# Four crossed groups per pair in the second FFN, with a new order of its steps

## The chip, the cores and the metric

One core of one Trainium2 chip runs the whole program in one launch. The metric is device time in microseconds (us). The kernel before has a median of 1088.23 us over 3 runs (1087.71 to 1088.48).

## The reference

```python
qn = q / (norm(q, axis=1) + 1e-6);  kn = k / (norm(k, axis=1) + 1e-6)
a  = softmax(kn.T @ qn / tau)            # 256 x 256
x  = v @ a                               # 6016 x 256
g  = x @ w_gate                          # first FFN, 256 -> 1536 -> 256
x  = (g * sigmoid(g) * (x @ w_val)) @ w_out
h  = x @ w_in                            # second FFN, 256 -> 2048 -> 256
y  = (h * clip(h + 3, 0, 6) / 6) @ w_out2
```

## The kernel before, in words

Attention is folded into the first FFN's weights, and both FFNs run transposed, with features on the partitions and tokens along the free dimension. Tokens go in six pairs of two blocks. In the second FFN (layer two) a block has 512 tokens in five pairs and 448 in the last. All products keep about fp32 precision by splitting each operand into a high and a low part: one product is three matmuls (`mm3`, L114: high by high, low by high, high by low).

**The forward products.** Layer two has 16 tiles of 128 hidden features, which are taken two at a time: eight groups (0 to 7) per pair. A group is a 2x2 block product (two feature tiles by two token blocks, over two halves of the 256 inputs), done by the Strassen-Winograd scheme in seven products instead of eight: 21 matmuls into three PSUM banks, `ps_a`, `ps_b` and `ps_d`. ScalarE (ACT) copies `ps_a` into `ps_b` (step AB) and two intermediate sums to SBUF (steps D, B). VectorE (DVE) adds into these (A22, A12). Then for each of the four results ACT takes relu(x+3) (R11, R21, R22, R12) and DVE a clip times x (K11, K21, K22, K12). That is 7 ACT and 6 DVE instructions. The next group's products wait for these banks: `ps_a` for K11, `ps_d` for A12, `ps_b` for K21; and within a group P6 and P2 wait for AB, P7 for B, P3 for D, P4 for A22.

**The back products.** Each result is split for the second matrix: ACT writes the high part (H), DVE the low part (L), both in a place `hl` or `hx`. In a *plain* group, four results each meet 2 output tiles: 4 items of 6 matmuls into the accumulators `o`. In a *crossed* group the back product is a Winograd scheme as well, 7 items of 3 matmuls: DVE makes four differences (D1 to D4; three stay in `xt`), and there are seven splits (P1 to P7). P2, P3 and P4 go into `o`. P1, P5, P6 and P7 go into a shared bank `al`, one kind after the other for all crossed groups of the pair: all P1, an ACT copy (step C) of the running sum, all P6, a copy, all P5, a copy, all P7, a copy. So this chain can only end after the last crossed group. Then two DVE sums, and four DVE outputs `xo` (L1761) with their stores.

So a plain group has 45 matmuls, 10 DVE and 11 ACT instructions; a crossed one 42 matmuls, 17 DVE and 14 ACT. Per pair there are also 2 DVE sums, 4 DVE outputs, 4 ACT copies, and (except in the last pair) the preparation of the next pair's operands with 11 DVE and 7 ACT instructions. Before, groups 1 and 4 are crossed.

**The order.** Tile placement and order are written out by the program itself at build time. In layer two every instruction is a `Step` with an engine, needs, a place it takes, and a due time; `run_steps` walks a clock per engine at fixed rates and lets the engine take the startable step that is due first. On TensorE (PE) it decides between the next forward product and a back item by the rules in `pick` (how crowded DVE is, how much back work is waiting). SP issues the DMAs in the order found. The weights of the forward products come by DMA from a DRAM copy into a ring of three tiles, each with two groups.

**Before layer two.** In layer one the second FFN's weights are split and written to DRAM (`second_steps`, one step of the conversion beside each group of layer one, mostly on POOL). A crossed group's rows of the last matrix need Winograd sums there.

Of the kernel before, what the change touches and what calls it, by code (L numbers as in the profile page):

```python
# [18 lines left out]
def channel_attention_then_two_ffns(  # L19
# [24 lines left out]
    nc = tc.nc  # L44
# [13 lines left out]
    CROSSED = (1, 4)  # L58
# [409 lines left out]
    with tc.manual_schedule():  # L468
# [381 lines left out]
        class Cube:  # L850
# [151 lines left out]
        def cross_tile(j):  # L1002
            return room["t"][:, j]
# [25 lines left out]
        def shared_copy(name, p, n):  # L1029
# [4 lines left out]
                "P6": ((0, 1), cross_tile(NQ - 1)[:, :n]),  # L1034
# [11 lines left out]
        def cross_back():  # L1046
# [4 lines left out]
            w = room["w"][:, i]  # L1051
# [65 lines left out]
        NG2I = NF2 // CT // 2  # L1117
# [8 lines left out]
        plain_f = [CT * i + j for i in range(NF2 // CT) if i not in CROSSED for j in range(CT)]  # L1126

        def load_w2o(fs, pool, tag, size):
            t = pool.tile([P, size, 2, C], F32R, tag=tag, name="w2o")
# [9 lines left out]

        def next_weights(g):  # L1140

            if g < RING:
                load_w2i(g)
            elif g == RING:
                load_w2o(plain_f[:NQ], w1_p, f"w{g}", NQ)
                t = const.tile([P, HALF, TB], F32R, tag="wo0", name="hx")
                room["hl"] = [t[:, CT * j : CT * (j + 1)] for j in range(HALF // CT)]
            elif g == 4:
                room["w"] = w1_p.tile([P, len(CROSSED), 2, NQ, P], F32R, tag=f"w{g}", name="w2x")
                nc.sync.dma_start(out=room["w"].bitcast(F32), in_=wx_d)  # L1150
            elif g == 5:
                room["t"] = w1_p.tile([P, NQ, TB], F32, tag=f"w{g}", name="xt")
            else:
                room["e"] = [e_p.tile([P, TB], F32, tag="e", name="xe") for _ in range(CT)]
                load_w2o(plain_f[NQ:], const, "wo1", HALF)
# [225 lines left out]

        RATE = {"PE": (1.25, 40, 170), "ACT": (1 / 1.2, 95, 190), "DVE": (1 / 0.96, 72, 80)}
        LANDS = {"weights": 9000, "raw": 5500, "store": 4500, "operand": 5500, "out": 4500}
        GAP, PE_GAP = 130, 300
        queues = {e: [] for e in ("PE", "ACT", "DVE", "SP")}

        class Step:
            def __init__(self, engine, due, run, needs=(), takes=None, gives=(), n=TB, cost=1, ahead=None):
                self.engine, self.due, self.run = engine, due, run
                self.needs = [x for x in needs if x]  # L1390
                self.takes, self.gives, self.n, self.cost, self.ahead = takes, gives, n, cost, ahead
                self.end = None
                queues[engine].append(self)

        class Place:

            def __init__(self, kind, make, after=()):
                self.kind, self.make, self.tile, self.after = kind, make, None, [x for x in after if x]
# [7 lines left out]
        spare = {"h": [], "hl": []}  # L1406

        def passed_by(x, engine, t):
            if x.end is None or x.engine == engine == "PE":
                return x.end is not None  # L1410
            return x.end + (0 if x.engine == engine else PE_GAP if engine == "PE" else GAP) <= t

        def place_of(step, t):
            return next((q for q in spare[step.takes] if all(passed_by(x, step.engine, t) for x in q.after)), None)

        def can_start(step, t):
            if not all(passed_by(x, step.engine, t) for x in step.needs):
                return False
            return not step.takes or place_of(step, t) is not None

        def pick(engine, t):
            found = [s for s in queues[engine][:120] if can_start(s, t)]
            if engine != "PE":
                return min(found, key=lambda s: s.due) if found else None
            forward = next((s for s in queues[engine] if s.ahead is not None), None)
            items = [s for s in found if s.ahead is None]
            if forward not in found:
                return min(items, key=lambda s: s.due) if items else None
            crowd = sum(1 for s in queues["DVE"][:120] if s.due < forward.due + SOON and can_start(s, t))
            if items and (crowd >= BUSY or sum(s.cost for s in items) >= MOST):  # L1430
                return min(items, key=lambda s: s.due)
            return forward

        SOON, BUSY, MOST = 20000, 2, 10

        def run_steps():
            clock = {e: 0 for e in queues}
            while any(queues.values()):
                engine = min((e for e in queues if queues[e]), key=lambda e: clock[e])
                t = clock[engine]  # L1440
                step = pick(engine, t)
                if not step:
                    clock[engine] += 40
                    assert t < 2_000_000, [(e, len(q)) for e, q in queues.items()]
                    continue
                queues[engine].remove(step)
                if step.takes:
                    place = step.place = place_of(step, t)
                    spare[step.takes].remove(place)
                    step.run(place.get())  # L1450
                else:
                    step.run()
                for other in step.gives:
                    place = other.place
                    place.after = [step]
                    spare[place.kind].append(place)
                if engine == "SP":
                    busy, more = 60, LANDS[step.n]
                else:
                    rate, fixed, more = RATE[engine]  # L1460
                    busy = (rate * step.n + fixed) * step.cost
                clock[engine] = t + busy
                step.end = t + busy + more
                step.began = t

        def layer2():
# [9 lines left out]

# [5 lines left out]
            def old_item(entry, needs=()):  # L1482
# [9 lines left out]
                step = Step("PE", -5000 + len(l1_items), run, needs, cost=2, n=prev.n)  # L1492
# [10 lines left out]
            def old_split(h, key, needs, due):  # L1503
# [9 lines left out]
                hi = Step("ACT", due, hi, [*needs, ring[-4], order[-1] if order else None], n=n1)  # L1513
                lo = Step("DVE", due + 1, lo, [hi], n=n1)
# [9 lines left out]
            def forward_step(run, needs, n, ahead):  # L1524
                forward[0] = Step("PE", state["base"], run, [forward[0], *needs], n=n, cost=1, ahead=ahead)
                return forward[0]


            def cube_steps(p, i, base):
                u, n = NP + p, pairs[p][1]  # L1530
                o = Step.__new__(Step)
                c = i if p or i else -1
                first = not (p or i)
                k = (NF2 // CT * p + i) // 2
# [42 lines left out]
                P1 = forward_step(make, [free["a"], op(0), wload.get(k)], n, 2)  # L1577
                AB = Step("ACT", base + 800, ab, [P1, free["b"]], n=n)
                P5 = forward_step(p5, [free["d"], op(1)], n, 0)
                if first:  # L1580
                    done4 = forward_step(lambda: prev.p4(), [], n1, 2)
                    times = Step("DVE", base + 2000, lambda: prev.times(prev.r11, prev.b), [done4], n=n1)
                    r11_lo = old_split(prev.r11, (0, 1), [times], base + 2500)
                    free["alpha"] = [times]
                    free["w5"] = Step("SP", 0, lambda: next_weights(prev.i // 2), [done4], n="weights")
# [8 lines left out]
                    free["wo1"] = Step("SP", 0, lambda: next_weights(NG1), done_old, n="weights")  # L1594
                D = Step("ACT", base + 1800, to("x22", "d"), [P5], takes="h", n=n)
                P6 = forward_step(product("b", S2, T2), [AB, op(2)], n, 2)
                B = Step("ACT", base + 3700, to("x12", "b"), [P6], takes="h", n=n)
                P2 = forward_step(product("a", A12, B21), [AB, op(3)], n, 2)
                R11 = Step("ACT", base + 6200, to("r11", "a", AF.Relu, bias=three), [P2], takes="h", n=n)
                K11 = Step("DVE", base + 7000, clip("r11", "a"), [R11], n=n)  # L1600
                P7 = forward_step(product("b", S3, T3), [B, op(5)], n, 0)
                A22s = Step("DVE", base + 6300, add("x22", "b"), [P7, D], n=n)
                P3 = forward_step(product("d", S4, B22), [D, op(4)], n, 2)
# [310 lines left out]
```

## Time and profile before

| | |
|---|---|
| median of 3 runs | 1088.23 us |
| profiled execution | 1087.67 us, span 1085.9 us |
| granted TensorE clock | 1.000 |
| layer two's first matmul | 598.2 us in the span |
| PE busy | 1077.6 us (99%) |
| DVE busy | 860.0 us (79%) |
| ACT busy | 777.5 us (72%) |
| POOL busy | 85.4 us (8%) |

In the trace a matmul's record is longer than the distance to the next one, because matmuls are pipelined: PE's rate is read from start to start. The same holds for DVE and ACT, whose records overlap a little. Layer two has line L114 for its matmuls, L1472 for ACT, L1475 and L1569 for DVE.

### The profile page before, as it was taken

The numbers are of one execution on the slowest core, as the hardware profiler recorded it, in microseconds if no ns is written. First come the engines' busy times: TensorE is split into PE (matmuls) and PEld (weight loads), VectorE is DVE, ScalarE is ACT, GpSimd is POOL, SyncE is SP. The second block draws the span as 40 slices with busy tenths as digits, with TensorE's granted clock in tenths as the row PEclk, the third lists the DMA queues.
The fourth block names the chain that finished last, engine by engine and source line by source line (L and its number), as shares of the span: only waits on it lengthen the run. The fifth ranks groups of instructions, "written<-read, shape, count | busy, mean of one in ns | idle before, by whom it ended". The sixth has DMA issues, their size and how long they took to land.

```text
span 1085.9 us, 14089 instructions
## 1 busy us (share of the span) xinstructions
PE 1077.6 (99%) x4876; PEld 908.4 (84%) x4876; DVE 860.0 (79%) x1407; ACT 777.5 (72%) x1373; POOL 85.4 (8%) x103
## 2 busy tenths in 40 slices
PE   9999999999999999999999999999999999999998
PEld 8888888888888888888888778888888788888897
DVE  7899995776776777777676797897897797897785
ACT  7877766677767767776765787687686787776774
POOL 0000000121412132122100000000000000000000
PEclk9999999999999999999999999999999999999999
DMA  9623203246336336336565775555564665464400
GB/s 361 227 87 130 78 1 115 76 147 243 124 135 229 134 132 245 134 115 229 190 233 196 286 277 177 206 212 208 201 242 165 234 221 185 189 220 160 168 1 34
DMA packets 68263, 188.61 MB, mean 174 GB/s; under 512 B 5600, under 2 KB 31712, under 8 KB 64736
## 3 DMA queue, kind: packets, MB, share of 16 engines
q1 hardware_dynamic: 67760, 187.09, 48.3%
q8 instruction: 38, 0.62, 0.2%
q10 hardware_dynamic: 432, 0.62, 0.2%
q14 instruction: 33, 0.27, 0.1%
HBM read 127.27 MB, written 60.42 MB: 173 GB/s over the span
## 4 chain that ended last, share of the span: by engine, by line
PE 93%; DVE 4%; ACT 1%; DMA 1%; issue 0%; SPq 0%; DVEq 0%; ACTq 0%
PE o L114 35%; PE ps_b L114 22%; PE ps_a L114 14%; PE ps_d L114 14%; PE s L585 4%; PE al L114 3%; DVE h L1569 1%; DVE hl L1475 1%; DMA x_d<-xo 1%; DVE h L1475 1%; ACT h L1472 1%; DMA x2r<-x_d 0%; PE ps_a L695 0%; DVE sp L1475 0%; PE ps_d L695 0%
## 5 line engine op out<-in xcount | busy, mean ns | idle before, releaser
L114 PE MATMUL o<-hl,wo 128*128 128x496 f32 (+1 forms) x864 | 215.8, 385 | 0.0
L114 PEld LDWEIGHTS o<-hl,wo 128*128 128x128 f32 x864 | 161.7, 188 | 29.4
L114 PE MATMUL ps_b<-op,w 128*128 128x496 f32 (+1 forms) x540 | 139.2, 384 | 0.0
L114 PE MATMUL o<-hl,w2o 128*128 128x512 f32 (+1 forms) x558 | 137.4, 386 | 0.0
L945 DVE TENSOR_TENSOR hl<-h,hl 128x496 fp32r<-128x496 f32 (+1 forms) x118 | 83.1, 704 | 56.6 <-ACT hl L880 56.0
L114 PE MATMUL ps_b<-op,w2i 128*128 128x512 f32 (+1 forms) x432 | 120.6, 387 | 2.7 <-ACT ps_b L1472 1.4
L114 PEld LDWEIGHTS o<-hl,w2o 128*128 128x128 f32 x558 | 104.8, 188 | 19.7
L114 PEld LDWEIGHTS ps_b<-op,w 128*128 128x128 f32 x540 | 101.4, 188 | 18.2
L1472 ACT ACTIVATE hl<-h 128x512 fp32r<-128x512 f32 (+2 forms) x134 | 81.8, 617 | 25.0 <-DVE h L1569 23.0
L114 PE MATMUL ps_a<-op,w 128*128 128x496 f32 (+1 forms) x360 | 99.2, 384 | 0.0
L114 PE MATMUL ps_d<-op,w 128*128 128x496 f32 (+1 forms) x360 | 99.2, 384 | 0.0
L1475 DVE TENSOR_TENSOR hl<-h,hl 128x512 fp32r<-128x512 f32 (+2 forms) x134 | 89.6, 675 | 11.1 <-ACT hl L1472 10.9
L114 PEld LDWEIGHTS ps_b<-op,w2i 128*128 128x128 f32 x432 | 80.4, 188 | 20.8 <-ACT ps_b L1472 3.2
L1472 ACT ACTIVATE h<-h,three 128x512 f32<-128x512 f32 (+1 forms) x96 | 67.2, 712 | 31.9 <-DVE h L1475 31.7
L884 DVE TENSOR_TENSOR h<-h,ps_d 128x496 f32<-128x496 f32 (+1 forms) x60 | 40.4, 674 | 50.9 <-PE ps_d L114 45.3
L880 ACT ACTIVATE h<-ps_b 128x496 f32<-128x496 f32 (+1 forms) x60 | 35.3, 588 | 63.3 <-PE ps_b L114 63.3
L114 PE MATMUL ps_a<-op,w2i 128*128 128x512 f32 (+1 forms) x288 | 79.8, 385 | 0.0
L114 PE MATMUL ps_d<-op,w2i 128*128 128x512 f32 (+1 forms) x288 | 79.7, 385 | 0.0
L114 PEld LDWEIGHTS ps_a<-op,w 128*128 128x128 f32 x360 | 67.6, 188 | 12.1
L114 PEld LDWEIGHTS ps_d<-op,w 128*128 128x128 f32 x360 | 67.6, 188 | 12.1
L114 PE MATMUL o<-hx,w2o 128*128 128x512 f32 (+1 forms) x306 | 75.9, 385 | 0.0
L880 ACT ACTIVATE hl<-h 128x496 fp32r<-128x496 f32 (+1 forms) x118 | 72.4, 614 | 3.2 <-DVE h L936 2.9
(185 smaller groups left out, 1930.5 us busy)
## 6 DMA issues: line engine op xcount, KB each, us to landing
w2i<-wi_d SPq DMA_DIRECT2D x24, 1792.0 KB, 7.4
op<-opd SPq DMA_DIRECT2D x35, 512.0 KB, 4.6
opd<-sp SPq DMA_DIRECT2D x28, 496.0 KB, 2.7
op<-opd SPq DMA_DIRECT2D x28, 496.0 KB, 5.5
opd<-sp SPq DMA_DIRECT2D x21, 512.0 KB, 3.2
raw<-in_moe_w_out SPq DMA_DIRECT2D x14, 512.0 KB, 4.2
opd<-st SPq DMA_DIRECT2D x14, 512.0 KB, 4.5
x2r<-x_d SPq DMA_DIRECT2D x10, 512.0 KB, 4.9
```

The lines of the kernel that those rows point to most:

```text
L114: nc.tensor.matmul(out, lhsT=w, rhs=x, start=first, stop=last, skip_group_check=True)
L585: nc.tensor.matmul(s_ps[c], lhsT=tk[:, j - chunks[i][0], c * P : (c + 1) * P], rhs=tq[:, j - chunks[i][0], :], start=(j == 0), stop=(j == ...
L880: nc.scalar.activation(out[:, : self.n], src[:, : self.n], AF.Copy)
L884: nc.vector.tensor_tensor(out=out[:, :n], in0=a[:, :n], in1=b[:, :n], op=ALU.add)
L945: nc.vector.tensor_tensor(out=hl[:, 1, :n], in0=h[:, :n], in1=hl[:, 0, :n].bitcast(F32), op=ALU.subtract)
L1472: nc.scalar.activation(out, src, func, **kw)
L1475: nc.vector.tensor_tensor(out=out, in0=a, in1=b, op=op)
L1569: nc.vector.scalar_tensor_tensor(out=r, in0=r, scalar=6.0, in1=getattr(o, x)[:, :n], op0=ALU.min, op1=ALU.mult)
```

## The change

Groups 1, 3, 5 and 6 of each pair are crossed, where 1 and 4 were. The differences `xt` have two weight places of layer one instead of one (14 tiles of one block, one of which also serves as a place for results). The ring of forward weights has three places of one group each, and the DMAs are of one group; the freed half places hold the crossed groups' back weights (so `w2i` and `w2o` in the order's rows are also the tiles of these). The order is found anew: on PE a forward product that can start is always taken first; ACT and DVE may wait up to 300 ns of the program's own clock for a step with an earlier due time; and each step's due time is the group's base time plus a number from a table by kind of step and group. In the last pair the `al` chain's due times are 12000 ns earlier. The two sums after the chain have changed places.

```diff
-    CROSSED = (1, 4)
+    CROSSED = (1, 3, 5, 6)
...
-                w = w_in[layer, i // 2 + (layer - 1) * p * (NF2 // CT // 2)]
-                self.w = w[:, i % 2]
+                self.w = w_in[1, i // 2][:, i % 2] if layer == 1 else w_in[2, NC2 * p + i]
...
-            return room["t"][:, j]
+            return room["t"][j]
...
-        def load_w2i(k):
-            g = k % NG2I
-            assert converted(2 * (2 * g + 1))
-            w_in[2, k] = w1_p.tile([P, 2, 2, NQ, P], F32R, tag=f"w{k % RING}", name="w2i")
-            nc.sync.dma_start(out=w_in[2, k].bitcast(F32), in_=wi_d[:, 2 * g : 2 * g + 2])
+        def load_w2i(c):
+            i = c % NC2
+            assert converted(2 * i)
+            w_in[2, c] = ring[c % RING]
+            nc.sync.dma_start(out=w_in[2, c].bitcast(F32), in_=wi_d[:, i])
...
+        DUE = {
+            "AB": (-102757, -385598, 42621, -85052, -98204, -86545, 40299, 36879),
+            "D": (-252753, 246291, 10775, -58700, -34230, 136474, -328131, 66842),
...
+        GAP, PE_GAP, WAIT, HASTE = 130, 300, 300, 3
+        SOONER = 12000
...
+                self.tag, base = due
+                self.due = base + DUE[self.tag[0]][self.tag[1]]
...
+                first = min(r[1] for r in ready)
+                if engine != "PE":
+                    wait = 0 if engine == "SP" else WAIT
+                    return min((r for r in ready if r[1] <= first + wait), key=lambda r: r[0].due + HASTE * (r[1] - first))
+                ready = [r for r in ready if r[1] <= first]
+                front = next((r for r in ready if r[0].forward), None)
+                return front or min(ready, key=lambda r: r[0].due)
...
-                if i % 2:
-                    last_w[k] = P4
+                last_w[k] = P4
...
-                t1, t2, t3 = [len(CROSSED) * m + cross for m in range(3)]
+                t1, t2, t3 = [1 + len(CROSSED) * m + cross for m in range(3)]
...
+                base -= SOONER * (p == NP - 1)
...
-                            L, I = sp(name, g(names[t - 1]), [ts[t - 1]], due, [], [copies[-1]], [ALPHA])
+                            L, I = sp(name, g(names[t - 1]), [ts[t - 1], before[j]], base, [], [copies[-1]], [ALPHA])
...
-                    g = (NF2 // CT * p + i) // 2 + RING
-                    if i % 2 and g < NG2I * NP:
-                        wload[g] = Step("SP", base, lambda g=g: load_w2i(g), [last_w[g - RING]], n="weights")
+                    g = NC2 * p + i + RING
+                    if g < NC2 * NP:
+                        wload[g] = Step("SP", (("old", 3), base), lambda g=g: load_w2i(g), [last_w[g - RING]], n="weights")
```

On DVE, in the second pair, a crossed group before (group 4), from its first clip of an SBUF result to its last difference but one:

```order
L1569 SCALAR_TENSOR_TENSOR h_5574<-h_5574,h_5533 128x512
L1569 SCALAR_TENSOR_TENSOR h_5478<-h_5478,h_5488 128x512
L1475 TENSOR_TENSOR hx_5247<-h_5574,hx_5247 128x512
L1569 SCALAR_TENSOR_TENSOR h_5552<-h_5552,ps_b_6454 128x512
L1475 TENSOR_TENSOR xt_5483<-h_5478,h_5517 128x512
L1475 TENSOR_TENSOR xt_5483<-h_5574,xt_5483 128x512
L1475 TENSOR_TENSOR xt_5483<-h_5574,h_5478 128x512
L1475 TENSOR_TENSOR hl_5648<-h_5552,hl_5648 128x512
L1475 TENSOR_TENSOR hl_5589<-xt_5483,hl_5589 128x512
L1475 TENSOR_TENSOR h_5552<-h_5552,xt_5483 128x512
```

The same engine in the second pair of the change, from the end of crossed group 5 into crossed group 6, which now follows it:

```order
L1654 SCALAR_TENSOR_TENSOR h_5519<-h_5519,ps_b_6627 128x512
L1563 TENSOR_TENSOR hl_5614<-h_5607,hl_5614 128x512
L1563 TENSOR_TENSOR hx_5271<-xt_5468,hx_5271 128x512
L1654 SCALAR_TENSOR_TENSOR xt_5507<-xt_5507,ps_a_6676 128x512
L1563 TENSOR_TENSOR h_5553<-h_5553,ps_b_6702 128x512
L1563 TENSOR_TENSOR hx_5271<-h_5519,hx_5271 128x512
L1563 TENSOR_TENSOR hl_5695<-xt_5507,hl_5695 128x512
L1563 TENSOR_TENSOR h_5501<-h_5501,ps_d_6683 128x512
L1654 SCALAR_TENSOR_TENSOR h_5567<-h_5567,h_5553 128x512
L1654 SCALAR_TENSOR_TENSOR h_5596<-h_5596,ps_b_6702 128x512
L1654 SCALAR_TENSOR_TENSOR h_5607<-h_5607,h_5501 128x512
L1563 TENSOR_TENSOR hx_5271<-h_5567,hx_5271 128x512
```

The rows are of one kind in both; what moved is that two groups with seven more DVE instructions each stand back to back, and that the low parts of the `al` chain come between the next group's adds and clips.

On PE, the end of the program before (the last forward product is the third row from the end):

```order
L114 MATMUL al<-hl,w2x 128x448 x3
L114 MATMUL al<-hx,w2x 128x448 x3
L114 MATMUL ps_b<-op,w2i 128x448 x3
L114 MATMUL ps_d<-op,w2i 128x448 x3
L114 MATMUL o<-hl,w2o 128x448 x6
L114 MATMUL o<-hx,w2o 128x448 x6
L114 MATMUL ps_b<-op,w2i 128x448 x3
L114 MATMUL o<-hx,w2o 128x448 x6
L114 MATMUL o<-hl,w2o 128x448 x18
```

And in the change, the last forward product (first row) and ten rows behind it:

```order
L114 MATMUL ps_b<-op,w2i 128x448 x3
L114 MATMUL o<-hx,w2o 128x448 x3
L114 MATMUL o<-hl,w2o 128x448 x6
L114 MATMUL al<-hl,w2o 128x448 x3
L114 MATMUL al<-hl,w2i 128x448 x3
L114 MATMUL o<-hl,w2o 128x448 x6
L114 MATMUL al<-hl,w2i 128x448 x3
L114 MATMUL al<-hx,w2i 128x448 x3
L114 MATMUL o<-hx,w2o 128x448 x6
L114 MATMUL o<-hl,w2o 128x448 x6
L114 MATMUL al<-hl,w2i 128x448 x3
```

After these come three more `al` rows of 3 and 15 matmuls into `o`: the end of the `al` chain now stands behind the last forward product, with 66 matmuls there instead of 24.

## Rows read from the trace of the kernel before

**Rows 1.** The page, busy time, share of the span and instructions of each engine

```profile
span 1085.9 us, 14089 instructions
PE 1077.6 (99%) x4876; PEld 908.4 (84%) x4876; DVE 860.0 (79%) x1407; ACT 777.5 (72%) x1373; POOL 85.4 (8%) x103
```

**Rows 2.** Busy time by stretch: the second pair, and the sum of all six

```profile
core 0: us, PE busy (x) PEld busy (x) DVE busy (x) ACT busy (x) POOL busy (x), PEclk, DMA share, GB/s
680.00:760.00 80.00, 80.00 (x354) 66.25 (x353) 68.56 (x112) 60.59 (x105) 0.00 (x0) 1.00 0.57 208
...
sum 482.00, PE 479.21 PEld 400.71 DVE 400.62 ACT 357.90 POOL 0.00; mean PE 79.87 PEld 66.78 DVE 66.77 ACT 59.65 POOL 0.00
```

**Rows 3.** PE in order of time: start us, us, what, idle before and its releaser

```profile
708.33 0.84 PE L114 MATMUL ps_a<-op,w2i 128*128 128x512 f32 x3
709.01 0.84 PE L114 MATMUL ps_d<-op,w2i 128*128 128x512 f32 x3
...
1065.71 0.77 PE L114 MATMUL ps_a<-op,w2i 128*128 128x448 f32 x3
1066.32 0.78 PE L114 MATMUL ps_d<-op,w2i 128*128 128x448 f32 x3
```

**Rows 4.** PE in order of time: all its waits in layer two

```profile
601.09 0.96 PE L114 MATMUL ps_b<-op,w2i 128*128 128x512 f32 x3 [0.66 <-ACT ps_b L1472]
626.16 0.98 PE L114 MATMUL ps_b<-op,w2i 128*128 128x512 f32 x3 [0.40 <-DVE h L1475]
...
854.41 0.96 PE L114 MATMUL ps_b<-op,w2i 128*128 128x512 f32 x3 [0.40 <-ACT ps_b L1472]
868.96 0.96 PE L114 MATMUL ps_b<-op,w2i 128*128 128x512 f32 x3 [0.66 <-DVE h L1475]
...
1015.77 0.88 PE L114 MATMUL ps_b<-op,w2i 128*128 128x448 f32 x3 [0.38 <-ACT ps_b L1472]
```

**Rows 5.** DVE in order of time: back-to-back instructions of 512 and of 448

```profile
638.34 0.68 DVE L1569 SCALAR_TENSOR_TENSOR h<-h,ps_b 128x512 f32<-128x512 f32 x1
638.94 0.69 DVE L1475 TENSOR_TENSOR x2r<-x2r 128x512 f32<-128x512 f32 x1
...
1074.28 0.61 DVE L1475 TENSOR_TENSOR h<-h,ps_d 128x448 f32<-128x448 f32 x1
1074.81 0.62 DVE L1569 SCALAR_TENSOR_TENSOR h<-h 128x448 f32<-128x448 f32 x1
```

**Rows 6.** Busy time by stretch: two stretches in which DVE is densest

```profile
698.00:738.00 40.00, 40.00 (x178) 33.13 (x177) 38.99 (x64) 33.30 (x59) 0.00 (x0) 1.00 0.63 234
608.00:650.00 42.00, 41.47 (x181) 33.39 (x180) 38.58 (x63) 32.77 (x59) 0.00 (x0) 1.00 0.74 267
```

**Rows 7.** Groups by line: ACT's high parts: count, busy us, mean ns, idle before

```profile
L1472 ACT ACTIVATE hl<-h 128x512 fp32r<-128x512 f32 (+2 forms) x134 | 81.8, 617 | 25.0 <-DVE h L1569 23.0 <-DVE h L936 2.1
```

**Rows 8.** DMA issues: count, KB each, median us from issue to landing

```profile
w2i<-wi_d SPq DMA_DIRECT2D x24, 1792.0 KB, 7.4
```

**Rows 9.** Busy time by stretch: layer one while weights are converted

```profile
300.00:530.00 230.00, 230.00 (x1047) 196.23 (x1046) 168.70 (x261) 162.05 (x297) 52.17 (x58) 1.00 0.48 168
```

**Rows 10.** All engines in order of time: a chain copy, and the end

```profile
1072.60 0.55 ACT L1472 ACTIVATE xe<-al 128x448 f32<-128x448 f32 x1 [0.52 <-PE al L114]
...
1077.87 3.81 PE L114 MATMUL o<-hl,w2o 128*128 128x448 f32 x18
...
1080.50 1.16 DVE L1761 SCALAR_TENSOR_TENSOR xo<-o,xe 128x448 f32<-128x448 f32 x2 [1.03 <-PE o L114]
...
1082.11 0.62 DVE L1761 SCALAR_TENSOR_TENSOR xo<-o,xt 128x448 f32<-128x448 f32 x1
```

**Rows 11.** Waits of DVE: who for whom, us in total, times, longest

```profile
DVE h L1569 <- ACT h L1472: 48.1, 44, 2.9
```

More of the change, by code (lines that the diff above doesn't have):

```diff
@@ L1050, in cross_back @@
             a, where = WAYS[name]
[L1051 removed]
+            w = room["w", i]
             s, first = acc(2, p, where)
@@ L1404, in get @@
                 return self.tile
[L1406 to L1432, printed above, removed]
@@ L1434, in channel_attention_then_two_ffns, with follows @@
-        SOON, BUSY, MOST = 20000, 2, 10
-        def run_steps():
[L1437 to L1446, printed above, removed]
+        def follows(x, engine):
+            if x.engine == engine == "PE":
+                return begun[x] + busy_time(x)
+            return over[x] + (0 if x.engine == engine else PE_GAP if engine == "PE" else GAP)
@@ L1452, in run_steps @@
                     step.run()
+                begun[step] = t
+                clock[engine] = t + busy_time(step)
+                over[step] = clock[engine] + (LANDS[step.n] if engine == "SP" else RATE[engine][2])
                 for other in step.gives:
[L1454 to L1464, printed above, removed]
+                    places[other].after = [step]
+                    spare[other.takes].append(places[other])
+                todo -= 1
+                for s in leads[step]:
+                    left[s] -= 1
+                    if not left[s]:
+                        open_[s.engine].append(s)
+                        open_[s.engine].sort(key=rank.get)
         def layer2():
@@ L1511, in lo @@
                     tt(o["hl"][:, 1, :n1], h[:, :n1], o["hl"][:, 0, :n1].bitcast(F32), ALU.subtract)
-                hi = Step("ACT", due, hi, [*needs, ring[-4], order[-1] if order else None], n=n1)
-                lo = Step("DVE", due + 1, lo, [hi], n=n1)
+                hi = Step("ACT", (("old", 1), due), hi, [*needs, ring[-4], order[-1] if order else None], n=n1)
+                lo = Step("DVE", (("old", 2), due), lo, [hi], n=n1)
                 order.append(hi)
@@ L1593, in cube_steps @@
                     done_old = [x for _, x in l1_items]
[L1594 to L1603, printed above, removed]
-                A12s = Step("DVE", base + 8400, add("x12", "d"), [P3, B], n=n)
-                P4 = forward_step(product("b", A22, T4), [A22s, op(6)], n, 0)
-                R21 = Step("ACT", base + 9200, to("r21", "b", AF.Relu, bias=three), [P4], takes="h", n=n)
@@ L1607, in cube_steps @@
-                K21 = Step("DVE", base + 9800, clip("r21", "b"), [R21], n=n)
-                R22 = Step("ACT", base + 8500, to("r22", "x22", AF.Relu, bias=three), [A22s], takes="h", n=n)
-                K22 = Step("DVE", base + 9000, clip("r22", "x22"), [R22], gives=[D], n=n)
-                R12 = Step("ACT", base + 10500, to("r12", "x12", AF.Relu, bias=three), [A12s], takes="h", n=n)
-                K12 = Step("DVE", base + 11000, clip("r12", "x12"), [R12], gives=[B], n=n)
+                    free["wo1"] = Step("SP", (("old", 0), 0), lambda: next_weights(NG1), done_old, n="weights")
@@ new lines, in cube_steps @@
+                    for j in range(1 + 3 * len(CROSSED), 2 * NQ):
+                        Place("h", lambda j=j: room["t"][j], [free["w5"]] if j >= NQ else [])
+                D = Step("ACT", (("D", i), base), to("x22", "d"), [P5], takes="h", n=n)
+                P6 = forward_step(product("b", S2, T2), [AB, op(2)], n)
+                B = Step("ACT", (("B", i), base), to("x12", "b"), [P6], takes="h", n=n)
+                P2 = forward_step(product("a", A12, B21), [AB, op(3)], n)
+                R11 = Step("ACT", (("R11", i), base), to("r11", "a", AF.Relu, bias=three), [P2], takes="h", n=n)
@@ new lines, in cube_steps @@
+                K11 = Step("DVE", (("K11", i), base), clip("r11", "a"), [R11], n=n)
+                P7 = forward_step(product("b", S3, T3), [B, op(5)], n)
+                A22s = Step("DVE", (("A22", i), base), add("x22", "b"), [P7, D], n=n)
+                P3 = forward_step(product("d", S4, B22), [D, op(4)], n)
+                A12s = Step("DVE", (("A12", i), base), add("x12", "d"), [P3, B], n=n)
+                P4 = forward_step(product("b", A22, T4), [A22s, op(6)], n)
+                R21 = Step("ACT", (("R21", i), base), to("r21", "b", AF.Relu, bias=three), [P4], takes="h", n=n)
@@ new lines, in cube_steps @@
+                K21 = Step("DVE", (("K21", i), base), clip("r21", "b"), [R21], n=n)
+                R22 = Step("ACT", (("R22", i), base), to("r22", "x22", AF.Relu, bias=three), [A22s], takes="h", n=n)
+                K22 = Step("DVE", (("K22", i), base), clip("r22", "x22"), [R22], gives=[D], n=n)
+                R12 = Step("ACT", (("R12", i), base), to("r12", "x12", AF.Relu, bias=three), [A12s], takes="h", n=n)
+                K12 = Step("DVE", (("K12", i), base), clip("r12", "x12"), [R12], gives=[B], n=n)
@@ L1656, in get, with late_room @@
                     return lambda: cross_tile(name) if isinstance(name, int) else getattr(o, name)
-                weights = [free["w5"]]
+                weights = [free["wo1"]] if cross == 3 else []
+                def late_room(j):
+                    return [free["w5"]] if j >= NQ else []
                 def weight_of(row):
```

192 lines of the change are left out of this document (119 added, 73 removed), and 55 rows, old and new, of the table DUE.

## The prediction

> **What bounds the kernel now.** I read the page's busy times first. PE is busy for 1077.6 of 1085.9 us, DVE for 79%, ACT for 72% [rows 1]. A busy PE is not yet a PE at its rate, so I looked at the distance from start to start: in layer two three matmuls of 512 columns take 0.68 us, 227 ns each, and three of 448 take 0.61 us, 203 ns each [rows 3]. Then I held the counts against the stretches. The second pair, 680 to 760 us, holds 354 matmuls; 354 x 0.2267 is 80.25 us, so PE runs there at its own rate from end to end [rows 2]. Its waits in layer two are five, together 2.50 us [rows 4]. A wait costs more than the row shows: the idle time is counted from the modelled end of the matmul before, some 0.16 us after the next one could have started (a single record's 0.84 - 2 x 0.227 = 0.39, less 0.227), and the triple behind it takes 0.96 us where 0.84 is usual. So each is 0.50 + 0.16 + 0.12 = 0.78 us, the five 3.9 us. PE binds, and what a matmul is worth is its distance to the next.
>
> The second engine is DVE: 400.6 us busy in the 482 us of layer two, 81 us idle [rows 2]. Its largest wait there is for ACT's relu, 48.1 us in 44 waits [rows 11]: it has nothing else to do in its order. The change takes from PE and gives to DVE, so this slack is what the forecast turns on.
>
> **What is removed from PE.** Two more crossed groups in each of six pairs, three matmuls fewer each: 36. Of these 30 have 512 columns and 6 have 448: 30 x 0.227 + 6 x 0.203 = 8.0 us, all on the path, since no other engine ends later in these stretches.
>
> Against this stands a rule of the Trainium skill (Perfetto Trace Analysis, Identifying the Most-Contended Engine): matmul busy time is no good measure of TensorE's distance to its limit, and the busy share of the weight loads is. The loads are busy for 66.25 of 80 us in the second pair, 83%, at 188 ns each [rows 2]. If that engine's limit were the loads, a removed matmul would be worth 188 ns, and the term 36 x 0.188 = 6.8 us. The start-to-start distance of 227 ns in an unbroken stretch says 8.0, and the measurement decides.
>
> **What is added to DVE and ACT.** A crossed group has seven DVE instructions more, so 84: 14 per pair, of which the first five have 512 columns at 0.60 us from start to start, the last 448 at 0.53 [rows 5]: 70 x 0.60 + 14 x 0.53 = 49.4 us. DVE then has 400.6 + 49.4 = 450 us of work in a layer that lasts 482 - 8 = 474 us: 95%, 24 us idle where it was 81. ACT has 36 more splits at 0.617 us [rows 7], 22 us, which makes 380 of 474, 80%; it stays third. All of this lies beside PE as long as DVE is in time; if the cover is gone, each microsecond in which DVE is late is one of PE's.
>
> Whether DVE can do this is bounded by two stretches. Per pair it has 112 instructions [rows 2] and will have 126 in about 78.6 us: 1.60 per us. From 698 to 738 us it had 64 in 40 us, also 1.60, was busy for 38.99 us, and PE was busy for all 40.00. From 608 to 650 us it had 63 in 42 us, and PE lost 0.53 us [rows 6]. By the first, the new waits are 0. By the second, 0.53 x 474 / 42 = 6.0 us of idle rows, and 0.78 / 0.50 of that is 9.4 us. Below 0 the term can't go, since all waits are then gone. The first stretch is the nearer in density; but it is short, and can live on back work piled up in the lighter groups ahead of it, which a layer that is dense throughout can't. The second comes right after the start of the layer, without such a pile. I take the middle, 4.7 us, where 3.9 is lost now: +0.8.
>
> **What is moved.** The order on the three engines is new as a whole. The rows on DVE show the two hardest groups, 5 and 6, back to back, and the chain's low parts among the next group's adds and clips. A clip late by one such instruction (0.60 us) makes `ps_a` or `ps_b` free that much later; behind it wait AB on ACT and then P6, P2 and P7 on PE, which cover it with a back item of 0.68 us if one is at hand. Taking forward products first leaves the items for such moments, but they now come in threes more often than in sixes. This is inside the term above.
>
> The end: four outputs and their stores follow the last matmul as now [rows 10]. Behind the last forward product there are now 66 matmuls, 66 x 0.203 = 13.4 us, with the rest of the chain in them. Between the last P5 item and the first P7 item stand 12 matmuls, 2.4 us, over a copy that took 0.55 us after a wait of 0.52 [rows 10]; behind the last P7 item 15 matmuls, 3.0 us, over a copy and two sums (0.5 + 0.55 + 2 x 0.62 = 2.3 us). Both are covered, the second by 0.7 us: 0, and at most 2 us if the copies come late.
>
> The ring on SP: a group's weights can be loaded once P4 of the group three before is done, so they have two groups, 19 us, to land. Loads of twice the size took 7.4 us [rows 8], so it is 0, with 12 us to spare; a load held in SP's order behind stores that wait for DVE would have to lose all of that first. If the cover were gone altogether, it would be up to 7.4 us.
>
> Layer one: 12 POOL and 4 ACT instructions more, beside the forward products. From 300 to 530 us POOL was busy for 52 of 230 us with 58 instructions, 0.90 us each, and PE lost nothing [rows 9]: 0. Exposed altogether it would be 12 x 0.9 = 10.8 us; a gain is excluded, since nothing goes from PE there.
>
> **The sum.** 1087.67 (the profiled execution: its span of 1085.9 and 1.8 around it) - 8.0 + 0.8 = 1080.5 us. That execution is 0.56 us below the median of its kernel, so a median after should be at about 1081.0, which is the forecast. All times below have this 0.56 in them. Less than 0.2% (2.2 us) can't be told from no change: faster is below 1086.0, slower above 1090.4.
>
> **Rivals.** *PE never waits.* If DVE is always in time and the table also removes the present waits, 3.9 us more come back: 1088.2 - 8.0 - 3.9 = 1076.3 us. For it speaks that three of six pairs have no wait now [rows 4]; against it that DVE had then 81 us of slack, and that the first pair waits at the start of the layer with 1.06 us of its rows' idle time, where the order has little choice.
>
> *The gain is eaten by waits.* Triples are half as long as the sixes which they replace: one wait of 0.78 us in each of the twelve added crossed groups is 9.4 us over the present ones: 1088.2 - 8.0 + 9.4 = 1089.6, no change. For it: all five waits are on `ps_b` products, and a triple covers 0.68 us, no more than one DVE instruction with its semaphores. Against: the crossed groups of now have the same triples, and there are twelve of them with five waits in all of layer two.
>
> *DVE becomes the bound.* Place: the clips of the crossed groups 5 and 6, which wait for ACT's relu in an order that can't give DVE anything else. Price: if the present waits for relu stay, 48.1 us, the layer lasts 450 + 48.1 = 498 us instead of 482: 1088.2 + 16 = 1104 us, slower. It decides from where DVE's idle time stays above 482 - 450 = 32 us; below 24 it costs nothing. For it: there is no room to catch up at 95%, and a step that comes late on DVE delays ACT, which delays DVE. Against: with work at hand DVE ran at 38.99 of 40 us [rows 6]; it waits for relu now because it has spare time.
>
> The same section of that page of the Trainium skill calls the engine with the highest occupancy the most contended, and takes occupancy as a fair measure for VectorE and the weight loads for TensorE. By that rule the change makes DVE, at 95% against 83%, the engine that binds, and this rival is what would follow. The stretch with DVE at 97% of its time and PE unbroken [rows 6] speaks against it.
>
> **How the numbers follow.** The forecast has 58%, PE without waits 14%, gain eaten 14%, DVE as bound 14%. The forecast's own range is 1077 to 1085.5: waits between 0.7 and 9.2 us. Faster are the first two, 0.72; no change is the third, 0.14; slower the fourth, 0.14. The range runs from 1076 us, where the first rival is taken in, to 1090 us, where the third is; the DVE-bound case and the end's or the ring's mishaps lie above.
>
> **What the profile after would show.** Matmuls fewer by 36 and the same 227 ns between starts; layer two's first matmul again at about 598 us; DVE with 84 more instructions and its idle time in layer two at 20 to 30 us; PE's waits in layer two few, each below 1 us, on `ps_b`. Waits for DVE that recur in groups 5 to 7 of each pair, with DVE busy before them, would show the DVE bound. Waits at each crossed group with DVE idle would show the triples too short. A matmul distance below 227 ns elsewhere, or a later start of layer two, would make the prediction wrong in a way that no part of it foresees.

## The result and the profile after

| | before | after |
|---|---|---|
| median | 1087.97 us (4 runs) | 1077.05 us (4 runs, 1076.27 to 1077.31) |
| ratio, 95% interval | | 0.9898 (0.9881 to 0.9916) |
| span of the profiled execution | 1085.9 us | 1075.3 us |

The change is faster by 10.9 us; the forecast had 7.2 us (1081.0 after 1088.23). The page after, with the lines that answer to [rows 1] and [rows 8]:

```profile
PE 1068.3 (99%) x4840; PEld 902.3 (84%) x4840; DVE 909.4 (85%) x1491; ACT 801.1 (75%) x1413; POOL 92.3 (9%) x115
...
w2i<-wi_d SPq DMA_DIRECT2D x48, 896.0 KB, 4.6
```

PE has 36 matmuls fewer (4876 to 4840), DVE 84 instructions more, ACT 40, POOL 12. Busy time by stretch, which answers to [rows 2]; the columns are the same:

```profile
598.00:680.00 82.00, 80.26 (x354) 65.68 (x353) 75.59 (x123) 64.93 (x113) 0.00 (x0) 1.00 0.67 241
680.00:760.00 80.00, 80.00 (x355) 66.26 (x354) 78.06 (x128) 65.26 (x113) 0.00 (x0) 1.00 0.58 211
...
842.00:922.00 80.00, 80.00 (x354) 66.26 (x354) 78.02 (x127) 65.94 (x114) 0.00 (x0) 1.00 0.61 216
...
sum 472.00, PE 470.26 PEld 395.15 DVE 451.03 ACT 381.23 POOL 0.00; mean PE 78.38 PEld 65.86 DVE 75.17 ACT 63.54 POOL 0.00
```

DVE is busy for 451 of 472 us, and in the second pair for 78.06 of 80, while PE starts 355 matmuls there: as many as the 354 at full rate before [rows 2]. The stretch from 842 to 922 us, most of the fourth pair, reads in the kernel before:

```profile
842.00:922.00 80.00, 78.94 (x347) 64.72 (x347) 67.64 (x111) 60.99 (x107) 0.00 (x0) 1.00 0.61 215
```

There PE started seven matmuls fewer in 80 us than the 354 of its full rate, 1.6 us lost; after, none. All waits of PE in layer two after, which answer to [rows 4] (PE in order of time):

```profile
601.82 0.96 PE L114 MATMUL ps_b<-op,w2i 128*128 128x512 f32 x3 [0.66 <-ACT ps_b L1560]
625.62 0.96 PE L114 MATMUL ps_b<-op,w2i 128*128 128x512 f32 x3 [1.08 <-DVE xt L1563]
```

Two where there were five, both in the first 28 us of the layer. And what DVE waits for there, answering to [rows 11] (us, times, longest):

```profile
DVE h L1654 <- ACT h L1560: 3.8, 12, 0.5
DVE hl L1563 <- ACT hl L1560: 3.7, 11, 0.7
DVE xt L1563 <- ACT xe L1560: 3.7, 1, 3.7
...
DVE xt L1654 <- ACT xt L1560: 1.3, 2, 0.8
```

The clips' waits for relu have gone from 48.1 us to 5.1: 3.8 in `h`, and 1.3 in `xt`, one place of which now holds results too. (The wait of 3.7 us for `xe` is at the very end, for the last chain copy.) DVE now has other work when a relu is not ready. Most of that comes with the added work itself: the same two rows add up to 33.6 us with two crossed groups and the new rules (run 1 below), and to 7.0 with four and plain offsets (run 2).

**Where the 10.9 us come from.** Layer two lasts from its first forward matmul to the end of the last matmul's record: 598.25 to 1077.87 + 3.81 us before, 483.43 us; 598.98 to 1070.76 + 0.77 after, 472.55 us. That is 10.9 us less; in this execution the layer starts 0.7 us later, and what lies behind its last matmul is 0.4 us shorter. The 36 matmuls are 8.0. The rest is waiting: 1770 matmuls of 512 at 0.2267, 354 of 448 at 0.2033 and 21 of 496 at about 0.22 are 477.85 us before, 1740, 348 and 21 are 469.83 us after. With 0.16 us taken off each total, as the last record outlasts its distance, 5.4 us were lost before and 2.6 us after. So of the 10.9 us the matmuls are 8.0 and the waits 2.9.

### The profile page after: what moved, and what is told of

Its sections match the earlier page's. It is cut to its first block, busy times and chain, and to the rows that moved or that the text cites. A ratio compares the mean times of both kernels' runs of the same rounds, so it can differ in the third digit from the quotient of the medians.

```text
span 1075.3 us, 14217 instructions
## 1 busy us (share of the span) xinstructions
PE 1068.3 (99%) x4840; PEld 902.3 (84%) x4840; DVE 909.4 (85%) x1491; ACT 801.1 (75%) x1413; POOL 92.3 (9%) x115
## 4 chain that ended last, share of the span: by engine, by line
PE 94%; DMA 4%; DVE 1%; ACT 1%; issue 0%; ACTq 0%; SPq 0%; DVEq 0%
PE o L114 34%; PE ps_b L114 23%; PE ps_d L114 15%; PE ps_a L114 15%; PE al L114 6%; DMA tk<-in_k 2%; DMA x_d<-xo 1%; DVE acc L607 1%; DMA tq<-in_q 1%; PE s L585 0%; DMA x2r<-x_d 0%; PE ps_a L695 0%; PE ps_d L695 0%; PE ps_b L695 0%; ACT ps_b L1560 0%
## 5 line engine op out<-in xcount | busy, mean ns | idle before, releaser
L114 PE MATMUL o<-hl,w2o 128*128 128x512 f32 (+1 forms) x405 | 101.4, 386 | 0.0
L114 PEld LDWEIGHTS o<-hl,w2o 128*128 128x128 f32 x405 | 76.1, 188 | 14.1
L1563 DVE TENSOR_TENSOR hl<-h,hl 128x512 fp32r<-128x512 f32 (+2 forms) x118 | 79.0, 675 | 3.6 <-ACT hl L1560 3.5
L1560 ACT ACTIVATE hl<-h 128x512 fp32r<-128x512 f32 (+2 forms) x118 | 72.6, 618 | 11.2 <-DVE h L1654 7.2
L879 ACT ACTIVATE ps_b<-ps_a 128x496 f32<-128x496 f32 (+1 forms) x60 | 34.2, 570 | 42.7 <-PE ps_a L114 42.7
L1560 ACT ACTIVATE h<-h,three 128x512 f32<-128x512 f32 (+1 forms) x75 | 52.5, 711 | 16.9 <-DVE h L1563 16.8
```

The costliest lines, as they stand in the source:

```text
L114: nc.tensor.matmul(out, lhsT=w, rhs=x, start=first, stop=last, skip_group_check=True)
L879: nc.scalar.activation(out[:, : self.n], src[:, : self.n], AF.Copy)
L1560: nc.scalar.activation(out, src, func, **kw)
L1563: nc.vector.tensor_tensor(out=out, in0=a, in1=b, op=op)
```

## The experiments

All times are medians. The kernel before, run beside each group of them, lay between 1087.8 and 1088.5 us, so a difference between runs of two groups can be off by some 0.7 us; where that matters, the layer's length in the profiled executions is given too. The runs keep the order that the changed kernel has where this is said; in the others the program finds it again.

**1. Two crossed groups, new rules.** The table's numbers are replaced by the offsets of the kernel before, one per kind.

```diff
-    CROSSED = (1, 3, 5, 6)
+    CROSSED = (1, 4)
...
-            "AB": (-102757, -385598, 42621, -85052, -98204, -86545, 40299, 36879),
+            "AB": (800, 800, 800, 800, 800, 800, 800, 800),
```

> The changed kernel with groups 1 and 4 crossed again, and in the table the due offsets that the kernel before had for each kind, the same for all groups; the new rules of choice, the ring of single groups and the new rooms stay. It has the 36 matmuls again. Theory A (the count of matmuls carries the gain, the order only the waits): 1085.0 us if the new rules alone remove the waits as in the changed kernel (1077.05 + 8.0), up to 1088 if the table was needed for that. Theory B (the new rules and the ring carry the gain, the crossed groups little): 1077 to 1080 us.

1086.37 us, ratio 0.998 (0.997 to 0.999): 2 of the 11 us come without the added crossed groups. It stands 9.3 us above the changed kernel, of which 8.0 are the matmuls; the remaining 1.3 fit its waits (four with 2.55 us in the rows, where the changed kernel has two with 1.74). Theory B falls.

**2. Four crossed groups, plain offsets.** The table replaced in the same way, with the four groups kept.

> The changed kernel with four crossed groups, but the due offsets of the kernel before by kind instead of the table. 36 matmuls fewer than before, DVE at 95%. Theory A with the table as a small matter: 1077 to 1081 us, DVE idle below 32 us in layer two. Rival (the table is what keeps DVE in time): DVE idle above 32 us, waits of PE at the crossed groups 5 and 6, 1088 us or more.

1082.81 us, 0.9948 (0.9933 to 0.9963): between the two cases, 5.8 us above the changed kernel. Four of its seven waits of PE, in order of time:

```profile
627.32 0.96 PE L114 MATMUL ps_b<-op,w2i 128*128 128x512 f32 x3 [0.70 <-DVE xt L1563]
...
773.77 0.96 PE L114 MATMUL al<-hl,w2i 128*128 128x512 f32 x3 [0.71 <-ACT xe L1560]
...
853.66 0.96 PE L114 MATMUL al<-hx,w2i 128*128 128x512 f32 x3 [0.71 <-ACT xe L1560]
...
933.54 0.96 PE L114 MATMUL al<-hl,w2i 128*128 128x512 f32 x3 [0.71 <-ACT xe L1560]
```

Three times, 80 us apart as the pairs are, the first item behind a chain copy is taken before the copy is done: 3 x 0.71, with what the rows hide (0.28 each, as in the prediction) 3 x 0.99 = 3.0 us. The table removes these three. The rest of the 5.8 us lies in the first pair (the first fence row and what stands around it) and in the last.

**3. The 36 matmuls back.**

```diff
                             mm3(s[:, :n], (w[:, 0, a, :], w[:, 1, a, :]), x, begin, True)
+                            if key == "P2" and cross in (1, 3):
+                                mm3(s[:, :n], (w[:, 0, a, :], w[:, 1, a, :]), x, False, True)
```

> The changed kernel, same order, with the three matmuls of item P2 issued twice in groups 3 and 6 of every pair (36 matmuls; these products are added twice, so the output is another one). Theory A (PE sets the pace of layer two, a matmul is worth its distance of 227 or 203 ns): 1077.05 + 8.0 = 1085.0 us, within 1. Rival (DVE sets the pace already, PE has room): below 1080 us.

1085.04 us, 0.9967 (0.9954 to 0.998), 8.0 above the changed kernel: 222 ns for a matmul, as the distance from start to start has it. In the profiled executions layer two lasts 480.5 us here against 472.5, and PE's waits are the same two, together 0.2 us longer. The Trainium skill's measure (Perfetto Trace Analysis, Identifying the Most-Contended Engine), by which the weight loads tell TensorE's distance to its limit, would have made it an estimated 6.8 us, as the prediction works it out. This run doesn't agree with it.

**4 and 5. More DVE work.** The low parts of one split (24 instructions) or two (48) of each plain group are written twice; the order stays.

```diff
-                        tt(hl[:, 1, :n], src()[:, :n], hl[:, 0, :n].bitcast(F32), ALU.subtract)
+                        for _ in range(2 if key in ((0, 0),) else 1):
+                            tt(hl[:, 1, :n], src()[:, :n], hl[:, 0, :n].bitcast(F32), ALU.subtract)
```

> The changed kernel, same order, with the low part of the first split of each plain group written twice (24 DVE instructions more, 20 x 0.60 + 4 x 0.53 = 14.1 us; the result is unchanged). DVE then has 465 us in 472. Theory A (DVE's idle 21 us is room that PE doesn't need): 1077 to 1080 us. Rival (DVE is at its edge, the idle rest can't be used): 14 us more, about 1091 us.

1083.94 us, 0.9959 (0.9944 to 0.9974): 6.9 us for an estimated 14.1 us of DVE work (the page's busy time rose by 12.3), between the two cases.

> As the run with 24 DVE instructions more, but 48 (the low parts of two splits of each plain group are written twice): 28.2 us more on DVE, 479 us of work where the changed kernel has 472 us of layer two. In that run 14.1 us on DVE cost 6.9 us, about half. Theory A (DVE's idle rest of 21 us is used up first, and from there each microsecond is one of the time): 1077.05 + 28.2 - 7.2 (what the first 14.1 us found covered) = 1098 us, so 14 us more than with 24. Rival (about half stays covered): 1077 + 13.8 = 1091 us.

1095.44 us, 1.007 (1.0055 to 1.0085): 11.5 us for the next 14.1, between its two cases as well. The layer's lengths in the profiled executions say the same: 472.5, 479.5 and 491.0 us. So the room ends gradually: half of the first portion is paid for, four fifths of the second. This holds for work put into a fixed order; whether an order found for it would hide more was not run. The second pair in the first of them, and PE in order of time there:

```profile
680.00:760.00 80.00, 79.72 (x349) 64.71 (x348) 78.86 (x130) 64.19 (x111) 0.00 (x0) 1.00 0.58 211
```

```profile
712.62 0.84 PE L114 MATMUL o<-hl,w2i 128*128 128x512 f32 x3
713.58 0.96 PE L114 MATMUL ps_b<-op,w2i 128*128 128x512 f32 x3
```

PE counts as busy for 79.72 of 80 us, but starts 349 matmuls where the changed kernel starts 355: 1.4 us lost, and only 0.28 shown as idle. The second fence has such a wait: 0.96 us between the starts of two triples where 0.68 is usual. The record of the triple before covers 0.16 of these 0.28 us; the 0.12 that are left stand in no row either, as the shortest idle time that a row shows here is 0.15.

**6. Four crossed groups with the old rules.** As 2, with the old choice on PE and no patience on ACT and DVE.

```diff
-        GAP, PE_GAP, WAIT, HASTE = 130, 300, 300, 3
+        GAP, PE_GAP, WAIT, HASTE = 130, 300, 0, 0
...
+                items = [r for r in ready if not r[0].forward]
+                if front and items:
+                    soon = [s for s in open_["DVE"] if s.due < front[0].due + 20000]
+                    crowd = sum(1 for s in soon if (start_of(s) or (first + 1,))[0] <= first)
+                    if crowd >= 2 or sum(r[0].cost for r in items) >= 10:
+                        return min(items, key=lambda r: r[0].due)
                 return front or min(ready, key=lambda r: r[0].due)
```

> Four crossed groups with the plain due offsets, as in the second run of the first call, and with the rules of choice of the kernel before as well (PE takes back items when two or more DVE steps are waiting or when items of ten units are at hand; ACT and DVE take the earliest due of what can start, with no patience). Theory A (the table does most, the rules little): 1082 to 1086 us. Rival (front products first and the patience carry the order): 1088 us or more, with DVE idle above 32 us in layer two.

1081.40 us, 0.9941 (0.9924 to 0.9957): no worse than 2. With plain offsets the new rules gain nothing; the table together with the new rules does, 4.4 us against this run. The table with the old rules was not run, so its share alone stays open. Pairs two to five run at full rate here too; the first loses most:

```profile
598.00:680.00 82.00, 78.85 (x341) 62.98 (x340) 74.20 (x121) 63.14 (x110) 0.00 (x0) 1.00 0.66 238
680.00:760.00 80.00, 80.00 (x354) 65.99 (x353) 76.78 (x127) 64.69 (x114) 0.00 (x0) 1.00 0.61 211
```

**7. The preparation on POOL.** The 55 instructions are `nc.gpsimd.tensor_tensor` in place of `nc.vector.tensor_tensor`.

> The changed kernel, same order, with the 55 DVE instructions that prepare the next pair's operands on POOL instead, which is idle in layer two: DVE has 55 x 0.60 = 33 us less. Theory A (PE is at its pace in the changed kernel, DVE in time): 1076 to 1077.5 us, PE's waits in layer two as now. Rival 1 (DVE's edge still costs PE time): 1074 to 1075.5 us. Rival 2 (POOL and DVE hinder each other, DVE's instructions get longer while POOL works): 1080 us or more, with DVE's two-input instructions above 0.7 us in these stretches.

1090.29 us, 1.0021 (1.0012 to 1.003), 13 us slower than the changed kernel (11 to 12 in the three of its ten executions that had a granted clock of 1.000) though DVE has 55 instructions fewer. DVE by line (count, busy us, mean ns), first in the changed kernel, then here:

```profile
L1563 DVE TENSOR_TENSOR hl<-h,hl 128x512 fp32r<-128x512 f32 (+2 forms) x118 | 79.0, 675 | 3.6 <-ACT hl L1560 3.5
L1654 DVE SCALAR_TENSOR_TENSOR h<-h 128x512 f32<-128x512 f32 (+1 forms) x75 | 49.7, 673 | 0.3 <-ACT h L1560 0.2
L1654 DVE SCALAR_TENSOR_TENSOR h<-h,ps_b 128x512 f32<-128x512 f32 (+1 forms) x45 | 30.2, 671 | 0.5 <-ACT h L1560 0.3
```

```profile
L1563 DVE TENSOR_TENSOR hl<-h,hl 128x512 fp32r<-128x512 f32 (+2 forms) x118 | 86.0, 735 | 4.4 <-ACT hl L1560 4.2
L1654 DVE SCALAR_TENSOR_TENSOR h<-h 128x512 f32<-128x512 f32 (+1 forms) x75 | 58.5, 790 | 1.8 <-ACT h L1560 1.8
L1654 DVE SCALAR_TENSOR_TENSOR h<-h,ps_b 128x512 f32<-128x512 f32 (+1 forms) x45 | 30.1, 668 | 0.6 <-ACT h L1560 0.3
```

Instructions with two SBUF inputs got longer, those with one input in PSUM did not. One place in order of time shows how, ending in the longest kind of PE wait in this run, 1.78 us:

```profile
716.05 1.74 POOL L1900 TENSOR_TENSOR st<-x2r,st 128x512 fp32r<-128x512 f32 x1
717.75 1.74 POOL L1913 TENSOR_TENSOR x2r<-x2r 128x512 f32<-128x512 f32 x1
```

```profile
716.56 1.77 DVE L1654 SCALAR_TENSOR_TENSOR xt<-xt,h 128x512 f32<-128x512 f32 x1
718.26 1.77 DVE L1654 SCALAR_TENSOR_TENSOR h<-h 128x512 f32<-128x512 f32 x1
...
721.30 0.97 PE L114 MATMUL ps_b<-op,w2i 128*128 128x512 f32 x3 [1.78 <-ACT ps_b L1560]
```

Two clips take 1.77 us instead of 0.67, each begun beside a POOL instruction of 1.74 and ending 0.54 us after it; the AB copy behind them is late, and P6 on PE behind that. The Trainium skill (SBUF — State Buffer, SBUF: two separate sides) says that a DVE instruction with two SBUF inputs and a GpSimd instruction that reads SBUF contend for a port pair, which the one that starts first holds for its whole length while the other is blocked. These rows agree. As this run holds back DVE, it can't tell whether a freer DVE would help; the next does.

**8. Less DVE work.** In pairs two to six; the order stays.

```diff
+                        m = 64 if p and key in ((0, 0), (1, 0)) else n
-                        tt(hl[:, 1, :n], src()[:, :n], hl[:, 0, :n].bitcast(F32), ALU.subtract)
+                        tt(hl[:, 1, :m], src()[:, :m], hl[:, 0, :m].bitcast(F32), ALU.subtract)
```

> The changed kernel, same order, with the low parts of two splits of each plain group written for the first 64 columns only, in pairs two to six (40 instructions; the other columns keep an older low part, so the output is another one in its last digits). From the distances of 0.60 us at 512 and 0.53 at 448 columns, 64 columns are estimated at 0.11: 32 x 0.49 + 8 x 0.42 = 19 us less on DVE. Theory A (in the changed kernel PE no longer waits for DVE after the first pair, so the curve of time against DVE work is flat on this side): 1076.3 to 1077.3 us. Rival (DVE already costs PE time in these pairs, in waits too short for the rows): 1074.5 to 1076 us.

1076.67 us, 0.9896 (0.9881 to 0.9911): the changed kernel's time within what can be told. DVE's sum over the same six stretches is 15 us lower (not 19: the shortened instructions have records of 0.22 us):

```profile
sum 472.00, PE 469.86 PEld 394.99 DVE 436.26 ACT 379.49 POOL 0.00; mean PE 78.31 PEld 65.83 DVE 72.71 ACT 63.25 POOL 0.00
```

So the time is flat from 436 us of DVE work to the changed kernel's 451, and rises from there (runs 4 and 5). Theory A holds.

**9. No crossed neighbours.** As 2, with `CROSSED = (0, 2, 4, 6)`.

> Four crossed groups with the plain due offsets and the new rules, as in the second run of the first call (1082.8 us), but groups 0, 2, 4 and 6, so that no two stand side by side. Theory A (what the table mends is not the neighbourhood of 5 and 6, but the first pair and the items behind the chain's copies): 1081 to 1084.5 us. Rival (the neighbours 5 and 6 are the dense place, as my third rival had it): below 1080 us.

1084.06 us, 0.9963 (0.9949 to 0.9977), no better than groups 1, 3, 5 and 6 with the same offsets (1082.81 us): with these offsets the neighbours are not the place.

**10 and 11. The longest wait left.** In the changed kernel, in order of time before the wait at 625.62 us:

```profile
623.61 0.63 ACT L1560 ACTIVATE st<-x2r 128x512 fp32r<-128x512 f32 x1 [1.78 <-DMA x2r<-x_d]
...
624.27 0.69 DVE L1563 TENSOR_TENSOR st<-x2r,st 128x512 fp32r<-128x512 f32 x1 [1.66 <-ACT st L1560]
...
624.88 0.68 DVE L1563 TENSOR_TENSOR xt<-xt,ps_b 128x512 f32<-128x512 f32 x1
...
625.62 0.96 PE L114 MATMUL ps_b<-op,w2i 128*128 128x512 f32 x3 [1.08 <-DVE xt L1563]
```

The chain reads upwards: P4 waits for A22, A22 stands on DVE behind a low part of the preparation, that waits for its high part on ACT, and ACT for the load of the second pair's input. In run 10 the closures of the first high and low part are kept and called with the next step of their chain; the cut shows the high part, the low one is done alike:

```diff
+                        if p == 1 and j == 0:
+                            o["hi"] = go
+                            return
+                        if "hi" in o:
+                            o.pop("hi")()
+                        go()
```

> The changed kernel, but the first preparation step of the second pair on ACT and on DVE, which waits for the load of x2r, is issued two ACT and eight DVE instructions later; all else keeps its order. Theory A (the 1.08 us wait of PE at 625.6 us comes from ACT and DVE standing behind that load): the wait is gone, its 1.08 us and the 0.28 around it: 1.1 to 1.4 us less than the changed kernel. Rival (P4 is late there because DVE is late anyway): the wait stays, at 0.5 us or more, and the time with it.

> The changed kernel once more, for the comparison on the same chip: 1077.05 us, within 0.6.

1077.12 us (0.9901, 0.9885 to 0.9918) for run 10 and 1076.89 us (0.9897, 0.9883 to 0.9912) for run 11: no gain of run 10 over run 11. But the wait moved, in run 10:

```profile
624.17 0.84 PE L114 MATMUL ps_b<-op,w2i 128*128 128x512 f32 x3
...
628.85 0.97 PE L114 MATMUL ps_b<-op,w2i 128*128 128x512 f32 x3 [0.44 <-ACT ps_b L1560]
```

P4 starts 1.3 us earlier than in run 11 (625.49 us) without a wait. Then PE waits for the next group's AB copy, and in short gaps before the triples at 631.76, 638.77 and 643.24 us that show no idle time. Added up from start to start these come to 1.5 us, as much as the wait of run 11 cost (1.4). ACT still stands before the second half of the same load (0.70 us, at 624.84); a relu behind it makes a clip wait for 1.09 us (at 626.74), and the AB copy is behind that. So the theory on the cause of this wait holds, but removing it at P4 brought nothing: here the delay of a load that two engines share came out at other places. No version here beats the changed kernel.

## Why the prediction was right

The measured 1077.05 us lies in the range, 3.9 us below the forecast. It is nearer to the first rival (PE never waits, 1076.3 us), to which I had given 14%, than to the forecast. That rival's time was met in part by luck: it had all of 3.9 us of waits come back, where 5.4 were there and 2.9 came back. The forecast's own account was right on the matmuls and had the waits move the wrong way.

- *What binds.* Right: run 3 puts the 36 matmuls at 8.0 us, as worked out from the starts.
- *DVE's work.* Right: 450 us of 474 were forecast, 451 of 472 measured, with ACT at 381 us where 380 stood.
- *The waits*, "4.7 us, where 3.9 is lost now: +0.8", is the term that was mis-sized: it came to -2.9 (2.6 after, 5.4 before). Both its numbers failed, for different reasons.
  - The present loss was read from rows with idle time. Waits too short to show in a row were missed, 1.5 us of the 5.4. Holding starts against distances in all pairs, as I did for the second, would have shown them. One of them, in the kernel before, PE in order of time:

```profile
650.14 0.84 PE L114 MATMUL o<-hl,w2x 128*128 128x512 f32 x3
651.06 0.97 PE L114 MATMUL al<-hl,w2x 128*128 128x512 f32 x3
```

  - 0.92 us from start to start, 0.24 more than three matmuls take, and no idle time in the row (0.16 of it are under the record of the triple before).
  - The coming loss was bounded above by the stretch from 608 to 650 us [rows 6], as an example of a dense DVE. The wait in it, at 626.16 us, stands after the change at 625.62, and run 10 shows its cause there: the load of x2r, not DVE's density. The kernel before had the same load in front of that wait: ACT stood before it for 1.47 us from 620.8 to 622.26, and DVE behind ACT, in order of time:

```profile
622.93 0.69 DVE L1475 TENSOR_TENSOR st<-x2r,st 128x512 fp32r<-128x512 f32 x1 [1.20 <-ACT st L1472]
```

  - The other stretch, nearer in density and without a wait, was the one to take; that it was "short, and can live on back work piled up" was an argument that no row carried. Throughout pairs two to five after the change PE runs at its rate with DVE at 97%, and run 8 shows that at this density DVE costs PE nothing.
- *The chain's end, the ring, layer one*, each taken at 0: no wait of PE in the profile after belongs to any of them, and the later start of layer two comes from before layer one, as shown below.
- *The DVE-bound rival.* It did not come, and run 9 speaks against its place. Its point of decision, DVE idle above 32 us, was not reached, with 21. But runs 4 and 5 show that the edge was near: 14 us more work on DVE, in the same order, takes back 6.9 of the 10.9 us. By the Trainium skill (Perfetto Trace Analysis, Identifying the Most-Contended Engine) the engine with the highest occupancy is the most contended, which would have made DVE, at 96%, the bound. Run 8 says that it was not yet.
- *What the order is worth* I did not price apart: with plain offsets the same groups gain 5.7 us (run 2) or 6.4 (run 6) over the kernel before, 4 to 6 us less than with the table.

The later start of layer two (0.7 us) was not forecast, and no experiment was made on it, but the traces show where it arises. PE in order of time, first before, then after:

```profile
40.76 0.95 PE L559 MATMUL ss<-ones,acc 128*128 128x1 f32 x8
```

```profile
41.36 1.02 PE L559 MATMUL ss<-ones,acc 128*128 128x1 f32 x8 [0.22 <-DVE acc L607]
```

So 0.6 of the 0.7 us are there before layer one begins. Runs 2 and 6, which differ from the changed kernel only in the table and the rules, have this matmul at 40.94 and 40.65 us, the changed kernel again at 41.23 (run 11): it scatters between executions, and the change is not shown to have a part in it.

## What to carry to other kernels

When one engine sets the pace, price removed work by its distance from start to start, and find what it loses by counting starts against that distance in equal stretches: waits of 0.2 to 0.3 us between two rows showed no idle time here, and longer ones 0.16 us less than their length. In this case a second engine could be given work up to 95% of the time, in an order that nearly always had something ready; 14 us more in the same order were paid for by half. Ask for each wait whether the second engine was late because it was dense or because it stood behind something else, as here behind a load: only runs that change its load can tell (runs 4, 5 and 8). And removing a wait at one place is no gain as long as what is behind it, here the late load, comes out at the next (run 10).

## What the runs showed of the hardware

POOL's `tensor_tensor` of 128x512 in fp32 took 1.3 us at best and 1.74 us in the place shown, and DVE instructions with two SBUF inputs beside it went from 0.67 to as much as 1.78 us, while those that read one input from PSUM stayed at 0.67 (run 7). So moving 55 instructions off DVE to POOL made the kernel 13 us slower.
